# Linear attention with a gated causal unit: two tiles of 128 tokens instead of four of 64 in the raw products, and paired transposes of q in one batch

## The chip, the cores and the metric

The kernel runs on one core of a Trainium2 chip. The metric is the device time of one execution in microseconds (us); lower is better. The engines of the core are TensorE (PE; its weight loads are shown apart as PEld), VectorE (DVE), ScalarE (ACT), GpSimd (POOL) and SyncE (SP), which here only issues transfers.

## The reference

Everything is fp32. Batch 8, 8 heads, 576 tokens, head size 64, model width 512, 5 taps of a causal convolution.

```python
kv = np.einsum('bhsd,bhse->bhde', k, v)
out = np.einsum('bhsd,bhde->bhse', q, kv)
rms = np.sqrt(np.mean(out * out, axis=-1, keepdims=True) + 1e-06)
x = out / rms * g_norm                      # then heads side by side: (8, 576, 512)
for k in range(5):
    gate_pre += conv_w[k] * xp[:, k:k + S, :]   # xp: x with 4 zero tokens ahead
gate = 1.0 / (1.0 + np.exp(-gate_pre))
val = x @ w_val
return gate * val @ w_out
```

Since there is no softmax, each head needs only its 64x64 matrix kv; the "raw products" are q times that matrix, before the norm.

## The kernel before

**Order of the work.** The whole program is a list of steps written out by hand (PLAN, lines 19 to 204). Each step is a small function called with the batch and an index, such as `raw_pair 4 3`, and each engine carries out its own instructions in the order of that list. Batches overlap: while the val and out products of one batch run, the kv products and raw products of the next stand between them. An engine waits where an operand, or the PSUM bank that a step writes, isn't ready. All PSUM tiles come from eight banks that are used in turn (`ps`).

**Attention, by batch.** `kv_product` (L440) forms kv on four 64x64 quarters of TensorE; `kv_copy` brings it to SBUF (L450 for batch 0, L453 for the others). In SBUF, `kvs[b % 2]` has heads 0 to 3 on partitions 0 to 63 and heads 4 to 7 on partitions 64 to 127; the index hp (0 to 3) names such a pair of heads, and r (0 or 1) the half of the partitions. q must stand with the head dimension on the partitions: the tile qT is 128 partitions (r, d) by hp by 576 tokens. Tokens are held in an order of 18 blocks n of 32: `(n t)`.

For batches 2 to 7, `turn_q` makes qT with VectorE transposes. For batches 0 and 1, `load_q_rows` loads rows (h t) on the partitions, `turn_q_rows` (L477) turns them on TensorE for four blocks at a time (index j, 0 to 4; the last has two blocks), and `sort_q` (L484) copies the result with ScalarE from PSUM into qT, one copy for each j. In `turn_q_rows`, the matmul for block n and half r has a 128x64 weight tile (rows of q) and the 128x128 identity as moving operand, and writes to partitions r\*64 to r\*64+63: two matmuls stand side by side on the two column halves of the array.

Batch 0 multiplies by a block-diagonal kv (`raw_whole`, L512, full 128x128 weights). The other seven use `raw_product` (L501), through `raw_pair` (two chunks of 128 tokens) and `raw_tail` (the last 64 tokens). For each hp, each chunk, each 64 tokens of it (half) and each r, a 64x64 piece of qT is the weight and the 64x64 kv the moving operand. Row half r picks the PSUM bank, token half the output partitions. So four matmuls use the four quarters of the array at once.

Then `square` (L531, L535) and `sums` (L544) form the sum of squares, `powers` (L552, GpSimd) the inverse root, `normalise` the scaled x (L561 with VectorE for batch 0, L571 with ScalarE later). x is turned into xT: by TensorE (`turn_x`, L583, then `keep_x`, L590) for batches 0 and 1 and the tails, by VectorE and transfers (`turn_blocks`, `move_blocks`) for the rest.

**The gated unit.** `gate_start`, `gate_tap` (L621) and `gate_end` form the gate from xT. The product with w_val is `val_product` (L633) in batches 0 and 1, and `val_fast` (L682) after that, which saves one multiplication in eight by sums of blocks. The output product is done likewise by `fast_product` (L774) with a tail in `out_product` (L720). The weights arrive as fp64 and are narrowed to fp32 by `narrow_weight` in eight numbered parts, parts 1 to 3 on ScalarE (L368, L370, L372) and the rest on VectorE (L363, L375, L380, L385, L389), among the steps of batches 0 and 1.

**The steps around the change for batch 1** stand in this order in the list (others between them left out):

```
turn_q_rows 1 2; turn_q_rows 1 0; turn_q_rows 1 3; ... sort_q 1 0; turn_x 0 3;
turn_q_rows 1 4; sort_q 1 2; turn_q_rows 1 1; keep_x 0 3; ... sort_q 1 3; ...
turn_x 0 4; ... turn_x 0 2; ... kv_product 1 0; ... keep_x 0 2; keep_x 0 4; ...
val_product 0 1 1; ... kv_product 1 1; ... val_product 0 3 1; ...
sort_q 1 4; kv_copy 1 1; sort_q 1 1; kv_copy 1 0; ... raw_pair 1 3
```

Of the kernel before, what the change touches and what calls it, by code (L numbers as in the profile page):

```python
# [15 lines left out]
P = 128  # L16
# [191 lines left out]
def kernel(  # L208
# [11 lines left out]
    nc = tc.nc  # L220
    B, H, S, D = q.shape
    C = H * D
    HP = H // 2
    NJ = S // P
# [3 lines left out]
    TB = 32  # L228
# [4 lines left out]
    HB = P // TB  # L233
# [5 lines left out]
    TURNED_X = 2  # L239
    FAST_VAL = 2  # L240
    FAST_OUT = 0
    ROOTS = {(0, 2): H + H // 2, (0, 1): 2 * H}
    GATES = 3
    GVS = 3
# [8 lines left out]
    def ps(shape, name):  # L253
        return psum.tile(shape, FP32, tag="bank", bufs=8, name=name)

    kvs = [const.tile([P, HP, D], FP32, name=f"kv{i}") for i in range(2)]
    kv_bd = const.tile([P, HP, P], FP32, name="kvbd")
    ident = const.tile([P, P], FP32, name="ident")
# [14 lines left out]
    qs = const.tile([P, 3, NB, D], FP32, name="qs")  # L273
# [22 lines left out]
    st = {}  # L296
# [100 lines left out]
    for jt in range(NK):  # L397
        cols = slice(jt * P, (jt + 1) * P)
# [56 lines left out]
    def new_qT(b):  # L455
        if ("qT", b) not in st:
            st["qT", b] = work.tile([P, HP, S], FP32, tag="qT", name=f"qT{b}")
        return st["qT", b]
# [9 lines left out]
    def size(c):  # L468
        return P if c < NJ else T

    def turn_q_rows(b, j):

        m = min(HB, NB - j * HB)
        pq = ps([P, HB, P], f"qTps{b}_{j}")
        for n in range(m):
            for r in range(2):
                nc.tensor.matmul(  # L477
                    pq[r * D:(r + 1) * D, n, :], qs[:, r, j * HB + n, :], ident[:], start=True, stop=True)
        st["pq", b, j] = pq

    def sort_q(b, j):

        m = min(HB, NB - j * HB)
        nc.scalar.copy(  # L484
            out=new_qT(b)[:].rearrange("p h (n t) -> p n h t", t=TB)[:, j * HB:j * HB + m],
            in_=st["pq", b, j][:, 0:m].rearrange("p n (h t) -> p n h t", t=TB))

    def raw_product(b, *chunks):


        banks = [ps([P, len(chunks), C // 2 if chunks[0] < NJ else P], f"raw{b}_{chunks[0]}_{r}") for r in range(2)]
        for n, c in enumerate(chunks):
            st["raw", b, c] = [bank[:, n] for bank in banks]
        for hp in range(HP):
            for c in chunks:
                for half in range(2) if c < NJ else (hp // 2,):
                    first = c * P + (half * D if c < NJ else 0)
                    for r in range(2):
                        rows, cols = slice(r * D, (r + 1) * D), slice(half * D, (half + 1) * D)
                        to = hp if c < NJ else hp % 2  # L500
                        nc.tensor.matmul(  # L501
                            st["raw", b, c][r][cols, to * D:(to + 1) * D],
                            st["qT", b][rows, hp, first:first + D], kvs[b % 2][rows, hp, :],
                            start=True, stop=True)

    def raw_whole(b, c):

# [8 lines left out]
    def raw_pair(b, c):  # L516
        raw_product(b, c, c - 1)

    def raw_tail(b):
        raw_product(b, NJ)  # L520

    def heads(c):
        return H if c < NJ else H // 2
# [23 lines left out]
    def root_range(b, c):  # L547
        return slice(FIRST[c], FIRST[c] + ROOTS.get((b, c), heads(c)))

# [252 lines left out]
    def store(i, c, queue=nc.sync, blocks=range(HB)):  # L802
# [5 lines left out]
    steps = {f.__name__: f for f in (  # L808
        load_half, load_q, load_q_rows, stage_weight, narrow_weight, turn_cw, keep_cw, start_warm, warm_up,
        kv_product, kv_copy, turn_q, turn_q_rows, sort_q, raw_whole, raw_pair, raw_tail, square, sums, powers, normalise,  # L810
        turn_x, keep_x, turn_blocks, move_blocks, halo, gate_start, gate_tap, gate_end, val_product, keep_val, gated,
        val_sums, x_sums, val_fast, val_keep, out_product, keep_out, weight_sums, token_sums, fast_product, fast_keep,
# [36 lines left out]
```

## Time and profile before

| | us |
|---|---|
| runs shown | 304.69, 306.4, 432.16 |
| median | 306.4 |
| span of the profiled execution | 304.6 |
| TensorE time in L501 (raw products, batches 1 to 7) | 18.7 |
| TensorE time in L477 (turning q, batches 0 and 1) | 11.0 |
| ScalarE span at L484 (sorting q): 10 copies | 0.34 to 0.60 each |

A line of the profile's groups reads: source line, engine, operation, output<-inputs, for TensorE the tile of the array as rows\*columns, then the shape, the count, and after the bar the busy time in us (overlaps counted once) and the mean duration of one instruction in ns; at the end the idle time just before these instructions and what ended it. A line of the timeline reads: start in us, length in us, engine, line, operation, and how many instructions were merged into it. Matmuls are pipelined, so one instruction's duration is longer than the distance between two. The share of the core's TensorE clock that was granted is 0.993 over the span; the two lower slices lie at the start:

```profile
PEclk9979999999999999999999999999999999999999
```

### The profile page before, as it was taken

What the parts mean: (1) busy time and instruction counts of PE and PEld (TensorE: products, weight loads), DVE (VectorE), ACT (ScalarE), POOL (GpSimd) and SP (SyncE); (2) the same over time, 40 slices, a digit from 0 to 9 for tenths busy, and PEclk for the clock granted to TensorE, in tenths of its full rate; (3) what the DMA queues carried; (4) which work ended last, traced back from release to release, by engine and by line L of the source; (5) the groups of instructions that cost most, each with busy time, mean ns of one, the idle gap of its engine ahead of it and who ended that gap; (6) DMA issues with size and microseconds to landing.
All of it is one profiled execution on the core that took longest, in us unless ns stands there. A gap on an engine that the chain in (4) does not pass through costs nothing.

```text
span 304.6 us, 8977 instructions
## 1 busy us (share of the span) xinstructions
PE 294.8 (97%) x3441; PEld 232.4 (76%) x3441; DVE 269.2 (88%) x474; ACT 193.7 (64%) x596; POOL 114.9 (38%) x127
## 2 busy tenths in 40 slices
PE   7899999999999999999999999999999999999993
PEld 7788778877787785777778757787878588888582
DVE  1169999999999999999999999999999999999612
ACT  1569989999768664884586547683787354535220
POOL 3027354406568217364338352345536631000000
PEclk9979999999999999999999999999999999999999
DMA  7999998088569756988689477927411621112423
GB/s 269 343 368 343 272 302 210 4 230 269 154 147 329 231 163 167 269 220 260 173 253 294 111 175 232 326 72 214 114 48 30 169 80 34 36 42 64 103 69 103
DMA packets 32074, 55.53 MB, mean 182 GB/s; under 512 B 6166, under 2 KB 14358, under 8 KB 32032
## 3 DMA queue, kind: packets, MB, share of 16 engines
q1 hardware_dynamic: 29520, 49.76, 55.7%
q0 software_dynamic: 1632, 3.17, 4.1%
q10 hardware_dynamic: 880, 2.03, 1.8%
q8 instruction: 27, 0.44, 0.6%
q14 instruction: 15, 0.12, 0.1%
HBM read 39.21 MB, written 9.44 MB: 160 GB/s over the span
## 4 chain that ended last, share of the span: by engine, by line
PE 89%; DVE 5%; DMA 2%; issue 1%; ACT 1%; DVEq 0%; ACTq 0%; SPq 0%
PE a L774 18%; PE cb L774 14%; PE va L682 13%; PE val L633 11%; PE vc L682 6%; PE kvps L440 6%; PE raw L501 5%; PE out L720 5%; PE vb L682 4%; PE qTps L477 4%; PE raw L512 2%; PE xTps L583 2%; DMA qs<-in_q_dram 2%; DVE gate L621 2%; DVE xs L667 1%
## 5 line engine op out<-in xcount | busy, mean ns | idle before, releaser
L552 POOL TENSOR_TENSOR rt<-ss,mhalf 128x8 f32<-128x8 f32 (+3 forms) x38 | 68.9, 1822 | 101.0 <-DVE ss L544 100.8
L621 DVE SCALAR_TENSOR_TENSOR gate<-xT,cwT,gate 128x576 f32<-128x576 f32 x128 | 101.8, 809 | 1.0
L571 ACT ACTIVATE x<-raw,rt 128x64 f32<-128x64 f32 x252 | 55.8, 351 | 7.2 <-POOL rt L552 4.2
L604 POOL DMA_DIRECT2D xT<-y x48 | 26.4, 557 | 25.5 <-DVE ot L784 14.0
L633 PE MATMUL val<-xT,wval 128*128 128x288 f32 x128 | 33.0, 411 | 0.0
L774 PE MATMUL a<-wsum,sums 128*128 128x256 f32 x128 | 32.4, 382 | 0.0
L628 ACT ACTIVATE gate<-gate 128x576 f32<-128x576 f32 x32 | 22.0, 692 | 11.7 <-DVE gate L621 11.4
L633 PEld LDWEIGHTS val<-xT,wval 128*128 128x128 f32 x128 | 23.5, 190 | 6.5 <-ACT xT L590 0.4
L544 DVE TENSOR_REDUCE ss<-sq 128x8 f32<-128x520 f32 (+1 forms) x40 | 24.7, 627 | 2.9 <-ACT sq L531 2.5
L774 PEld LDWEIGHTS a<-wsum,sums 128*128 128x128 f32 x128 | 24.0, 190 | 4.1 <-issue 0.6
L535 ACT ACTIVATE sq<-raw 128x256 f32<-128x256 f32 (+1 forms) x70 | 22.4, 403 | 7.3 <-PE raw L501 7.1
L682 PE MATMUL va<-xs,vsum 128*128 128x288 f32 x96 | 26.6, 409 | 0.0
L615 ACT ACTIVATE gate<-xT,cwT 128x576 f32<-128x576 f32 x32 | 25.2, 811 | 1.5 <-DVE gv L646 1.3
L646 DVE TENSOR_TENSOR gv<-gv,gate 128x576 f32<-128x576 f32 x32 | 23.6, 750 | 0.9 <-ACT gate L628 0.8
L682 PEld LDWEIGHTS va<-xs,vsum 128*128 128x128 f32 x96 | 18.0, 190 | 5.1 <-ACT x L571 0.4
L611 POOL COPY xT<-xT 128x124 f32<-128x124 f32 x32 | 17.5, 585 | 10.5 <-ACT xT L590 10.5
L501 PEld LDWEIGHTS raw<-kv,qT 64*64 64x64 f32 x1008 | 16.4, 134 | 5.3 <-issue 3.0
L440 PEld LDWEIGHTS kvps<-v,k 64*64 64x64 f32 x1008 | 15.9, 135 | 3.7 <-issue 1.9
L501 PE MATMUL raw<-kv,qT 64*64 64x64 f32 x1008 | 18.7, 221 | 0.0
L440 PE MATMUL kvps<-v,k 64*64 64x64 f32 x1008 | 17.6, 220 | 0.0
L774 PE MATMUL cb<-wsum,sums 128*128 128x256 f32 x64 | 16.9, 386 | 0.1
L774 PE MATMUL cb<-wout,gv 128*128 128x256 f32 x64 | 16.8, 385 | 0.0
(111 smaller groups left out, 542.3 us busy)
## 6 DMA issues: line engine op xcount, KB each, us to landing
qs<-in_q_dram SPq DMA_DIRECT2D x96, 140.0 KB, 4.2
out_dram<-ot SPq DMA_DIRECT2D x140, 64.0 KB, 1.7
k<-in_k_dram SPq DMA_DIRECT2D x14, 576.0 KB, 6.3
v<-in_v_dram SPq DMA_DIRECT2D x12, 576.0 KB, 6.5
xT<-y SPq DMA_DIRECT2D x48, 64.0 KB, 2.7
xT<-y POOLq DMA_DIRECT2D x48, 64.0 KB, 3.3
y<-in_moe_w_val_dram SPq DMA_DIRECT2D x4, 512.0 KB, 11.4
w_wout<-in_moe_w_out_dram SPq DMA_DIRECT2D x4, 512.0 KB, 6.3
```

Source lines behind the costliest of these rows:

```text
L440: nc.tensor.matmul(st["kvps", b][s][r * D:(r + 1) * D, i], st["k", b, i][rows, r, cols], st["v", b, i][rows, r, cols], start=(j == 0), sto ...
L501: nc.tensor.matmul(st["raw", b, c][r][cols, to * D:(to + 1) * D], st["qT", b][rows, hp, first:first + D], kvs[b % 2][rows, hp, :], start=T ...
L544: nc.vector.reduce_sum(out=st["ss", b][:, FIRST[c]:FIRST[c] + n], in_=st["sq", b, c][:, 0:n], axis=AX.X)
L552: nc.gpsimd.tensor_tensor(out=st["rt", b][:, which], in0=st["ss", b][:, which], in1=mhalf[:, which], op=ALU.pow)
L571: nc.scalar.activation(out=x[:, to * D:(to + 1) * D], in_=raw[:, h * D:(h + 1) * D], func=AF.Copy, scale=root[:, to:to + 1])
L604: (nc.sync if i % 2 else nc.gpsimd).dma_start(out=xTs[b % 2][i * TB:(i + 1) * TB, :, first:first + P], in_=y[a * TB:(a + 1) * TB, i])
L615: nc.scalar.activation(out=gate[:], in_=xTs[b % 2][:, jt, HALO:SX], func=AF.Copy, scale=cwT[:, K - 1, jt:jt + 1])
L621: nc.vector.scalar_tensor_tensor(out=gate[:], in0=xTs[b % 2][:, jt, tap * TB:tap * TB + S], scalar=cwT[:, tap, jt:jt + 1], in1=gate[:], op ...
L633: nc.tensor.matmul(val[:], wval[:, kc, jt * P:(jt + 1) * P], xTs[b % 2][:, kc, HALO + n * SV:HALO + (n + 1) * SV], start=(kc == 0), stop=( ...
L646: nc.vector.tensor_tensor(out=both, in0=both, in1=st["gate", b, jt][:], op=ALU.mult)
L682: nc.tensor.matmul(st[bank, "val", b, mj][:], weights_[:, k], tokens()[:, k], start=(n in (0, 1, 3) and k == 0), stop=(k == NK // 2 - 1), ...
L774: nc.tensor.matmul(st[bank, i, p], tokens()[:, k], weights_[:, k], start=(n < 2 and k == 0), stop=(k == NK // 2 - 1), skip_group_check=True)
```

## The change

Two things change. The list of steps, its order and everything else stay.

In `raw_product`, a chunk of 128 tokens no longer takes two weight tiles of 64x64 for each r but one of 64x128 (64 partitions, 128 tokens). It lies on a tile of the array of half the height and the full width; two such tiles, r = 0 and r = 1, fill the array. Outputs, banks and the moving operand are the same. The tail of 64 tokens keeps its 64x64 tiles.

In `turn_q_rows` and `sort_q`, batch 1 takes another way: two neighbouring blocks n and n+1 of one r, 128 columns together, are turned by one 128x128 transpose. Its result has the even block on partitions 0 to 63 and the odd one on 64 to 127, for either r. So `sort_q` makes four copies, for each r and each parity, each from 64 partitions of PSUM to 64 partitions of qT, where it was one copy of 128 partitions.

```diff
+    PAIRED_Q = (1,)
...
-        pq = ps([P, HB, P], f"qTps{b}_{j}")
+        st["pq", b, j] = pq = ps([P, HB, P], f"qTps{b}_{j}")
+        if b in PAIRED_Q:
+            for r in range(2):
+                for n in range(0, m, 2):
+                    nc.tensor.transpose(
+                        pq[:, r * 2 + n // 2, :],
+                        qs[:, r, j * HB + n:j * HB + n + 2, :].rearrange("p n d -> p (n d)"), ident[:])
+            return
...
-        nc.scalar.copy(
-            out=new_qT(b)[:].rearrange("p h (n t) -> p n h t", t=TB)[:, j * HB:j * HB + m],
-            in_=st["pq", b, j][:, 0:m].rearrange("p n (h t) -> p n h t", t=TB))
+        qT, pq = new_qT(b)[:].rearrange("p h (n t) -> p n h t", t=TB), st["pq", b, j][:].rearrange(
+            "p n (h t) -> p n h t", t=TB)
+        if b not in PAIRED_Q:
+            nc.scalar.copy(out=qT[:, j * HB:j * HB + m], in_=pq[:, 0:m])
+            return
+        for r in range(2):
+            for e in range(2):
+                nc.scalar.copy(
+                    out=qT[r * D:(r + 1) * D, j * HB + e:j * HB + m:2],
+                    in_=pq[e * D:(e + 1) * D, r * 2:r * 2 + m // 2])
...
-                for half in range(2) if c < NJ else (hp // 2,):
-                    first = c * P + (half * D if c < NJ else 0)
-                    for r in range(2):
-                        rows, cols = slice(r * D, (r + 1) * D), slice(half * D, (half + 1) * D)
-                        to = hp if c < NJ else hp % 2
-                        nc.tensor.matmul(
-                            st["raw", b, c][r][cols, to * D:(to + 1) * D],
-                            st["qT", b][rows, hp, first:first + D], kvs[b % 2][rows, hp, :],
-                            start=True, stop=True)
+                first, to = c * P, hp if c < NJ else hp % 2
+                half = slice(0, P) if c < NJ else slice(hp // 2 * D, (hp // 2 + 1) * D)
+                for r in range(2):
+                    rows = slice(r * D, (r + 1) * D)
+                    nc.tensor.matmul(
+                        st["raw", b, c][r][half, to * D:(to + 1) * D],
+                        st["qT", b][rows, hp, first:first + size(c)], kvs[b % 2][rows, hp, :],
+                        start=True, stop=True)
```

More of the change, by code (lines that the diff above doesn't have):

```diff
@@ L478, in turn_q_rows @@
                     pq[r * D:(r + 1) * D, n, :], qs[:, r, j * HB + n, :], ident[:], start=True, stop=True)
-        st["pq", b, j] = pq
     def sort_q(b, j):
         m = min(HB, NB - j * HB)
-        nc.scalar.copy(
-            out=new_qT(b)[:].rearrange("p h (n t) -> p n h t", t=TB)[:, j * HB:j * HB + m],
-            in_=st["pq", b, j][:, 0:m].rearrange("p n (h t) -> p n h t", t=TB))
+        qT, pq = new_qT(b)[:].rearrange("p h (n t) -> p n h t", t=TB), st["pq", b, j][:].rearrange(
[8 more added lines that the diff above has]
+                    in_=pq[e * D:(e + 1) * D, r * 2:r * 2 + m // 2])
     def raw_product(b, *chunks):
```

## The prediction

> **What bounds the kernel now.** I read the page's busy time first, then its chain of waits.
>
> ```profile
> PE 294.8 (97%) x3441; PEld 232.4 (76%) x3441; DVE 269.2 (88%) x474; ACT 193.7 (64%) x596; POOL 114.9 (38%) x127
> ...
> PE 89%; DVE 5%; DMA 2%; issue 1%; ACT 1%; DVEq 0%; ACTq 0%; SPq 0%
> ```
>
> TensorE (PE) is busy for 97% of the span and is 89% of the chain. The windows view agrees: from 38 to 300 us PE is busy 260.60 of 262.00 us. So a microsecond that PE gains or loses counts fully, unless PE then waits. Both edits are PE edits: L501 (raw products) and L477 (turning q), with their copies on ScalarE (ACT) at L484.
>
> Next, the groups by line with shapes kept apart, because the change alters shapes (tile rows*columns, then operand):
>
> ```profile
> L501 PE MATMUL raw<-kv,qT 64*64 64x64 f32 x1008 | 18.7, 221 | 0.0
> L501 PEld LDWEIGHTS raw<-kv,qT 64*64 64x64 f32 x1008 | 16.4, 134 | 5.3 <-issue 3.0 <-ACT gv L642 0.8 <-DVE gv L689 0.4
> L720 PEld LDWEIGHTS out<-wout,gv 128*64 128x64 f32 x64 | 4.2, 136 | 8.0 <-issue 8.0
> L774 PEld LDWEIGHTS cb<-wout,gv 128*128 128x128 f32 x64 | 11.8, 190 | 2.1 <-ACT ot L788 0.2
> ```
>
> One fp32 matmul is two instruction pairs (load, matmul): 7 batches x 72 matmuls x 2 = 1008. A load of 64 columns takes 134 or 136 ns whether it has 64 rows or 128; one of 128 columns takes 190. The duration follows the columns, not the rows: 54 ns more for 64 more columns.
>
> How often can loads follow each other? The first loads after a change of tile shape show it, because nothing hides them. Three short stretches of the timeline (start us, us, engine, line, count):
>
> ```profile
> 89.02 0.30 PEld L774 LDWEIGHTS cb<-wout,gv 128*128 128x128 f32 x2
> 117.35 0.19 PEld L501 LDWEIGHTS raw<-kv,qT 64*64 64x64 f32 x5 [0.33 <-issue]
> 28.21 0.20 PEld L583 LDWEIGHTS xTps<-ident,x 128*128 128x128 f32 x2 [0.17 <-issue]
> ```
>
> Subtract the last load's duration from each stretch. The second 128-column load starts 0.30 - 0.19 = 0.11 us after the first. On quarters, four loads start almost together, and the fifth (the first tile's second) 0.19 - 0.13 = 0.06 us after the first. A transposing load (L583; mean 141 ns) brings 128 columns at 0.20 - 0.14 = 0.06 us.
>
> Last, how fast whole rounds run, a round being one instruction on every tile of the array (timeline of PE):
>
> ```profile
> 117.35 1.16 PE L501 MATMUL raw<-kv,qT 64*64 64x64 f32 x64
> 180.16 2.09 PE L501 MATMUL raw<-kv,qT 64*64 64x64 f32 x128
> 21.74 1.73 PE L512 MATMUL raw<-kvbd,qT 128*128 128x128 f32 x14
> ```
>
> Sixty-four more instructions, 16 rounds of four, take 2.09 - 1.16 = 0.93 us: 58 ns a round. With full-size weights and 128 moving columns (L512), (1.73 - 0.275)/13 = 112 ns each, 0.275 being one matmul's duration in that run. Streaming alone: 256 moving columns at L774 take 0.86 us for four on the chain, 216 ns each, or 0.84 ns a column, so 54 ns for 64 columns. A quarter round thus sits just above both its stream (54) and its load (55 to 60).
>
> **Raw products.** Per row pair and chunk there were 4 matmuls on 4 quarters, now 2 on 2 half-height tiles. Each instruction still streams 64 columns of kv, and two half tiles fill the array as four quarters did. So the number of rounds stays: 7 batches x 4 pairs x 4 chunks x 2 passes = 224 (896 quarter instructions divided by 4; the other 112 are the 64-token tail, which is unchanged). What changes is the load under each round: 128 columns instead of 64. It no longer fits under 54 ns of streaming, and the load sets the pace. No row shows a 64x128 load. From below a round is bounded by the stream, 54 ns; from above by two loads after each other, 2 x 107 + 5 = 219 ns. I take 112, the L512 row, where a load of the same number of columns runs at its own pace under a matmul no longer than it; the 64-row and 128-row loads of equal duration say that height doesn't help, and the quarter loads, starting together, that two tiles load side by side. Cost: 224 x (112 - 58) = +12.1 us, on PE, with no cover: PE has no waits in or right behind these stages that could absorb it.
>
> The Trainium skill has a rule for the height that no row measures directly, in "TensorE: Matmul & The Clock Gate", section "LDWEIGHTS (loading the stationary operand)": a load takes its columns divided by 1.2 GHz, and "A 32×128 weight load takes the same time as a 128×128 weight load". By it a round is 107 ns and the sum 224 x (107 - 58) = +11.0 us; it speaks against this change, and the pitches above (0.11 and 0.06 us) agree with it.
>
> **Turning q of batch 1.** Before: 36 matmuls, 72 instructions, 36 rounds of two. Rate, from the timeline of PE:
>
> ```profile
> 23.40 2.84 PE L477 MATMUL qTps<-ident,qs 128*64 128x128 f32 x48
> 26.17 0.66 PE L583 MATMUL xTps<-ident,x 128*128 128x128 f32 x4
> 26.75 1.53 PE L477 MATMUL qTps<-ident,qs 128*64 128x128 f32 x24
> 28.22 0.87 PE L583 MATMUL xTps<-ident,x 128*128 128x128 f32 x6
> ```
>
> (2.84 - 1.53)/12 = 109 ns a round, 3.9 us in all. Full transposes as in L583 need one instruction each; six take 0.87 us, (0.87 - 0.28)/5 = 0.12 us at most. The change has 18 of them: 2.0 us. It also removes three changes of tile shape around L583, about 0.15 us each (the chain gives the 24 rounds 2.77 us where 24 x 0.109 = 2.62). PE is relieved of 2.0 + 0.4 = 2.4 us.
>
> I don't expect PE to keep it. After these steps PE turns x of batch 0, which VectorE (DVE) normalises late:
>
> ```profile
> 27.45 0.42 DVE L561 TENSOR_TENSOR x<-raw,rt 128x256 f32<-128x256 f32 x1
> ...
> 29.06 1.29 DVE L561 TENSOR_TENSOR x<-raw,rt 128x512 f32<-128x512 f32 x2 [0.19 <-POOL rt L552]
> ```
>
> The x of chunk 4, the next to be turned, is ready at 27.87 (PE turned it at 28.22), and chunks 0 and 1 at 29.75 and 30.35, after roots from POOL that none of this moves; PE turned them from 30.23 on. So at 30.35 the 2.4 us have become waiting.
>
> And ACT pays. Five copies become twenty, each of half the partitions and half the elements per partition. Copies of 512 in a row take 0.49 us each (two in 1.07, one is 0.58). A copy of 256 takes 0.35 alone and one of 128 takes 0.26 (L450's 64x128 rows; 128x128 at L453 takes as much, so half the partitions save nothing). What decides is whether they overlap. On 128 partitions they do: two of 256 at L535 take 0.66, one 0.40, so 0.26 in a row. The only copies that alternate between the halves of the partitions are L450's:
>
> ```profile
> 16.56 1.09 ACT L450 COPY kvbd<-kvps 64x128 f32<-64x128 f32 x4 [1.51 <-PE kvps L440]
> ```
>
> Four in 1.09 us are 0.27 each, a whole duration: no overlap (one of them also waited for PE). With overlap the sorts cost 4 x (4 x 0.26 - 0.49) + (4 x 0.16 - 0.26) = +2.6 us, without 4 x (4 x 0.355 - 0.49) + (4 x 0.27 - 0.26) = +4.5. I take the second, as its row is the nearest in form. ACT is busy 2.87 of the 3.00 us from 30 to 33, so little of it hides. Three of these sorts stand before ACT's copies of x (L590), with one idle gap of 0.37 us:
>
> ```profile
> 26.86 0.60 ACT L590 ACTIVATE xT<-xTps 128x512 f32<-128x512 f32 x1 [0.37 <-PE xTps L583]
> 27.36 0.58 ACT L484 COPY qT<-qTps 128x512 f32<-128x512 f32 x1
> ...
> 29.97 2.04 ACT L590 ACTIVATE xT<-xTps 128x512 f32<-128x512 f32 x4
> ```
>
> 3 x 0.93 less the gap moves 29.97 to 32.4. Chunks 2 and 4, the first two of the four copies, end near 33.3, and the val product that needs them, begun at 31.16, is 2.1 us late. The exponent steps of the wval weights stand in the same queue; DVE's merge that waits for them (L375 at 30.27) slips by as much, inside PE's new delay. The last two sorts (+0.82 and +0.93) move the second kv copy, which ended at 35.46, to 39.4, and raw_pair 1 3, which PE began at 36.54 and would now reach at 38.6, waits for it until 39.4. I book +2.8 us on the path (with overlap the same steps give +1.0); bounds: -2.4 (all PE's relief kept) and +4.5 (all of ACT's extra).
>
> **Sum.** Own span 304.6 us, which is also the fastest shown run (304.69); the median is 1.8 us above. 304.6 + 12.1 + 2.8 = 319.5; I say 319, as the overlapping copies would give 317.7; that is 4.1% above the median.
>
> **Rivals.**
> - *Not slower: the half tile's load stays under the stream.* Place: L501's rounds; it decides once two 64x128 loads take under 58 ns. For: the transposing loads bring 128 columns every 60 ns, and each half tile holds only half the weights. Against: ordinary 128-column loads come every 107 ns, and a 64-row load isn't shorter than a 128-row one. Then the raw term is nil and ACT's delay remains: 304.6 + 2.8 = 307.4 us. Chance 0.09.
> - *The cost is per instruction.* If a quarter round's 58 ns were four fixed costs, half the instructions would need half; but rounds still stream 54 ns, so at most 224 x 4 = 0.9 us is won: 306.5 us with ACT's delay. Against: within a round the four start together, and two instructions on half-width tiles take 109 ns, their stream. Chance 0.02. A page names such a cost: the Trainium skill, "TensorEngine Tiling (Array Packing)", "Instruction Overhead", about 60 cycles for each matmul however small. By it four take 100 ns at the 2.4 GHz that the skill's TensorE page gives, and the measured 58 disagrees.
> - *Worse: loads lose their cover or queue for each other.* Load and stream in turn: 107 + 54 = 161 ns, +23 us, 330 us; one load after the other: 219 ns, +36 us, 343 us. Against: in all three shapes in the rows load and stream overlap. Chance 0.05.
>
> **How the numbers follow.** The forecast has 0.84. Its range: 304.6 + 12.1 - 2.4 = 314 up to 306.4 + 12.1 + 4.5 = 323, the upper end from the median run. It leaves out 0.16 in the rivals, and little more, so I keep it. Faster by over 2% (6 us; about what a measurement of this kernel can tell from no change) needs the relief kept and loads hidden, even then 302: 0.01. Within 2%, the two rivals: 0.11. Slower: 0.88.
>
> **What would show it.** L501 should have 560 instructions, 448 of them 64*128 with loads near 190 ns and rounds of two near 112 ns; a stage of 64 instructions that took 1.16 us becomes one of 32 near 2.0 us. L477 keeps batch 0's 72, and 18 transposes appear; ACT has 20 copies of batch 1, near 0.355 us apart (0.26 if they overlap), and PE waits before the val product and raw_pair 1 3. I am wrong if 64*128 loads come every 60 ns, or if PE is early at raw_pair 1 3.

## The result, and the profile after

The changed kernel takes 317.38 us (median of 4 runs, 316.67 to 318.26), the kernel before 305.54: the ratio is 1.0393 [1.0358, 1.0429], slower. Of the four runs of the kernel before (304.67, 304.69, 306.4 and 432.16 us), the last, a slow one, is left out of the ratio; without it their median is 304.69, and the change costs 12.7 us. The profiled execution has a span of 315.3 us and took 317.07.

The page after, busy time and chain of waits:

```profile
PE 301.8 (96%) x2939; PEld 241.0 (76%) x2939; DVE 270.8 (86%) x474; ACT 197.4 (63%) x611; POOL 114.8 (36%) x127
...
PE 81%; DMA 7%; ACT 7%; SPq 1%; issue 1%; DVE 0%; ACTq 0%; DVEq 0%
```

TensorE (PE) runs 502 instruction pairs fewer and is busy 7 us longer. ScalarE (ACT) is now 7% of the chain instead of 1%; the transfers (DMA) are 7% instead of 2%, for loads of q and v. The groups by line, shapes kept apart (raw products are now at L514, turning by transposes at L479, the sort at L498):

```profile
L514 PE MATMUL raw<-kv,qT 64*128 64x64 f32 x448 | 27.4, 274 | 0.4 <-ACT kv L454 0.4
L514 PEld LDWEIGHTS raw<-kv,qT 64*128 64x128 f32 x448 | 25.9, 188 | 4.4 <-issue 2.0 <-ACT kv L454 1.2 <-ACT x L584 0.4
L479 PE MATMUL qTps<-ident,qs 128*128 128x128 f32 x18 | 3.0, 323 | 1.4 <-ACT qT L498 1.4
L498 ACT COPY qT<-qTps 64x256 f32<-64x256 f32 x16 | 5.8, 365 | 0.2
```

A load of the new shape takes 188 ns, as long as the 128x128 loads of before (190): half the rows save nothing. The rate of rounds is in PE's timeline (start, length, engine, line, count):

```profile
122.83 2.00 PE L514 MATMUL raw<-kv,qT 64*128 64x64 f32 x32
...
188.35 3.79 PE L514 MATMUL raw<-kv,qT 64*128 64x64 f32 x64
```

Thirty-two more instructions, 16 rounds of two, take 3.79 - 2.00 = 1.79 us: 112 ns a round, where the quarters had 58. How often a load can start is seen at the head of such a stage, in PEld's timeline up to the third load:

```profile
122.83 0.29 PEld L514 LDWEIGHTS raw<-kv,qT 64*128 64x128 f32 x3 [0.33 <-issue]
```

The first two, one on each tile, start together, and the third, the first tile's second, 0.29 - 0.19 = 0.10 us after them (108 ns in the trace). So the two tiles load side by side, and each takes nearly a whole round for its 128 columns. Now the turning of batch 1, PE and then ACT:

```profile
20.65 1.47 PE L479 MATMUL qTps<-ident,qs 128*128 128x128 f32 x12
22.57 0.63 PE L596 MATMUL xTps<-ident,x 128*128 128x128 f32 x4 [0.45 <-ACT sq L544]
...
24.59 1.52 PE L479 MATMUL qTps<-ident,qs 128*128 128x128 f32 x6 [1.38 <-ACT qT L498]
26.11 1.54 PE L596 MATMUL xTps<-ident,x 128*128 128x128 f32 x6
...
31.27 2.21 PE L646 MATMUL val<-xT,wval 128*128 128x288 f32 x8 [0.86 <-ACT xT L603]
...
37.26 2.41 PE L514 MATMUL raw<-kv,qT 64*128 64x64 f32 x48 [0.43 <-ACT kv L454]
```

```profile
23.04 3.02 ACT L498 COPY qT<-qTps 64x256 f32<-64x256 f32 x8
...
26.58 1.49 ACT L498 COPY qT<-qTps 64x256 f32<-64x256 f32 x4
...
30.35 1.85 ACT L603 ACTIVATE xT<-xTps 128x512 f32<-128x512 f32 x4
...
36.94 0.27 ACT L454 COPY kv<-kvps 128x128 f32<-128x128 f32 x1
```

PE turns q faster and then waits three times for ACT: at 24.59 for a PSUM bank that the sort copies must free, at 31.27 for xT, at 37.26 for the kv copy. (The wait at 22.57 is put down to ACT too, but VectorE (DVE) wrote the x that PE turns there until 22.43.) From 21.48 to 37.22 us the chain of waits runs through ACT alone. Eight copies take 3.02 us; less the last one's 0.37 that is (3.02 - 0.37)/7 = 0.38 us from start to start, so they don't overlap.

Where the time went is read from the start of the same PE step in both timelines. The kernel before has, beside the turning of q that the prediction shows:

```profile
31.16 2.11 PE L633 MATMUL val<-xT,wval 128*128 128x288 f32 x8
...
36.54 1.44 PE L501 MATMUL raw<-kv,qT 64*64 64x64 f32 x80
```

| step | before | after | later by |
|---|---|---|---|
| first turning of batch 1 | 23.40 | 20.65 | -2.7 |
| first val product of batch 0 | 31.16 | 31.27 | +0.1 |
| raw_pair 1 3 | 36.54 | 37.26 | +0.7 |
| end of the span | 304.6 | 315.3 | +10.7 |

So the stretch from the turning to raw_pair 1 3 took 16.61 us instead of 13.14: +3.5. From there on each of the 14 raw_pair steps adds 0.84 us, 11.8 together. Some 1.8 us are given back in pieces of 0.05 to 0.3 us, in small waits of the kernel before (at 63.8, 143 and 157 us, for instance). The head of before's profile happened to be late, part of it because the clock was halved from 17.3 to 20.8 us (the 7 in before's clock line, its only lower slice). The sum: 304.6 - 2.7 + 3.5 + 11.8 - 1.8 = 315.4, against a span of 315.3.

### The profile page after: what moved, and what is told of

Same layout as the page of the kernel before. It is cut to its first block, busy times and chain, and to the rows that moved or that the text cites. A ratio compares the mean times of both kernels' runs of the same rounds, so it can differ in the third digit from the quotient of the medians.

```text
span 315.3 us, 7982 instructions
## 1 busy us (share of the span) xinstructions
PE 301.8 (96%) x2939; PEld 241.0 (76%) x2939; DVE 270.8 (86%) x474; ACT 197.4 (63%) x611; POOL 114.8 (36%) x127
## 4 chain that ended last, share of the span: by engine, by line
PE 81%; DMA 7%; ACT 7%; SPq 1%; issue 1%; DVE 0%; ACTq 0%; DVEq 0%
PE a L787 18%; PE cb L787 13%; PE va L695 13%; PE val L646 9%; PE raw L514 9%; PE vc L695 6%; PE kvps L441 5%; PE out L733 5%; DMA qs<-in_q_dram 4%; PE vb L695 4%; DMA v<-in_v_dram 3%; ACT qT L498 2%; PE xTps L596 1%; ACT wexp_wval L369 1%; ACT xT L603 1%
## 5 line engine op out<-in xcount | busy, mean ns | idle before, releaser
L514 PEld LDWEIGHTS raw<-kv,qT 64*128 64x128 f32 (+1 forms) x560 | 28.3, 177 | 5.8 <-issue 3.4
L514 PE MATMUL raw<-kv,qT 64*128 64x64 f32 (+1 forms) x560 | 30.6, 265 | 0.4 <-ACT kv L454 0.4
L624 POOL COPY xT<-xT 128x124 f32<-128x124 f32 x32 | 17.3, 581 | 13.6 <-ACT xT L603 13.6
L787 PE MATMUL a<-wsum,gv 128*128 128x256 f32 x64 | 16.7, 384 | 0.0
L797 DVE TENSOR_TENSOR ot<-cb,ot 128x512 f32<-128x512 f32 x16 | 10.9, 682 | 6.8 <-DMA out_dram<-ot 4.1
```

What stands on the lines that cost most here:

```text
L514: nc.tensor.matmul(st["raw", b, c][r][half, to * D:(to + 1) * D], st["qT", b][rows, hp, first:first + size(c)], kvs[b % 2][rows, hp, :], s ...
L787: nc.tensor.matmul(st[bank, i, p], tokens()[:, k], weights_[:, k], start=(n < 2 and k == 0), stop=(k == NK // 2 - 1), skip_group_check=True)
```

## The experiments

Theory: the round is paced by its 128-column load, and ACT's separate copies set the turning section. Rivals: the stream or a fixed cost sets the round; the turning costs by its relief or by something else.

**raw_only: the half-height products alone.**

```diff
-    PAIRED_Q = (1,)
+    PAIRED_Q = ()
```

> The raw products on half-height tiles alone; q of batch 1 is turned and sorted as before. Theory (a 128-column load sets the round at 112 ns instead of 58): 448 instructions on 64*128 with loads near 190 ns, a stage of 32 of them near 2.0 us instead of 1.16 us for 64, +10 to +12 us over before (about 315 to 317 us). Rival (most of the loss comes from the turning and sorting of q): less than +5 us, under 311 us.

Measured: 315.9 us against 305.06, ratio 1.0376 [1.0313, 1.0439], +10.8 us, as expected. The raw products are the main cost. Behind the head, PE's timeline also has one long stall that no engine explains (in brackets: the wait ahead and its releaser; "issue" is none):

```profile
109.75 0.42 PE L514 MATMUL raw<-kv,qT 64*64 64x64 f32 x7
111.57 0.45 PE L514 MATMUL raw<-kv,qT 64*64 64x64 f32 x9 [1.40 <-issue]
```

**wide_moving: the changed kernel with 128 columns streamed instead of 64** (for hp 0 to 2; the surplus half is overwritten).

```diff
+                    w = 2 if c < NJ and hp < HP - 1 else 1
...
-                        st["raw", b, c][r][half, to * D:(to + 1) * D],
-                        st["qT", b][rows, hp, first:first + size(c)], kvs[b % 2][rows, hp, :],
+                        st["raw", b, c][r][half, to * D:(to + w) * D],
+                        st["qT", b][rows, hp, first:first + size(c)],
+                        kvs[b % 2][rows, hp:hp + w, :].rearrange("p h e -> p (h e)"),
```

> As the changed kernel, but for row pairs 0 to 2 each raw matmul of a full chunk streams 128 columns of kv instead of 64 (this pair's and the next one's; the next pair's own matmul then overwrites the surplus), so 168 of 224 rounds stream twice as much under the same load. Theory (the load paces the round): streaming 107 ns still fits under it, rounds stay near 112 ns, the time equals the changed kernel's 317 us within 1 us. Rival (streaming, or writing columns into two banks, paces a round on half-height tiles): 168 x 54 ns = +9 us, 326 us.

Measured: 318.26 us, ratio 1.0428 [1.0391, 1.0464]. The stage of 64 instructions, 48 of them with twice the columns, is unchanged to the last digit:

```profile
92.34 3.79 PE L515 MATMUL raw<-kv,qT 64*128 64x128 f32 x64
```

Twice the streaming is free, so the stream doesn't set the round; the load does. The profiled execution is 1.5 us longer than the changed kernel's, and all of that lies ahead of the raw products: raw_pair 1 3 starts at 38.78 instead of 37.26, and from there to the end both take 278.0 us (316.8 - 38.78 and 315.3 - 37.26).

**sort_parts: when do ACT's copies overlap?** The kernel before, with batch 1's five full copies cut up in three ways.

```diff
+        parts = {
+            (1, 0): ((low, 0), (low, 2), (up, 0), (up, 2)),
+            (1, 2): ((low, 0), (up, 0), (low, 2), (up, 2)),
+            (1, 1): ((whole, 0), (whole, 2))}.get((b, j))
...
+        for (p0, p1), n in parts:
+            nc.scalar.copy(out=qT[p0:p1, j * HB + n:j * HB + n + 2], in_=pq[p0:p1, n:n + 2])
```

> The kernel before, with three of batch 1's five sorting copies cut into parts of two blocks: j=0 in the order lower half, lower, upper, upper of the partitions; j=2 lower, upper, lower, upper; j=1 on all 128 partitions, two copies. Theory (copies overlap unless the range of partitions changes): starts 0.26 us apart within a range and on 128 partitions, 0.36 us where the range changes. Rival 1 (copies of 64 partitions never overlap): 0.36 us throughout j=0 and j=2. Rival 2 (they overlap as any others and the sorts of the changed kernel were slow for another reason, the crossing of halves or the strided output): 0.26 us throughout.

Measured, from start to start in the trace: low after low 256 ns, up after up 272, whole after whole 264; but low to up 379, up to low 392, and alternating 378, 378 and 377. In ACT's timeline, cut after the second and after the third copy of the first way:

```profile
23.95 0.62 ACT L496 COPY qT<-qTps 64x256 f32<-64x256 f32 x2
...
23.95 1.00 ACT L496 COPY qT<-qTps 64x256 f32<-64x256 f32 x3
```

The second copy adds 0.26 us to the first's 0.36, the third, which changes to the other partitions, 0.38. Copies overlap by about 0.11 us unless the range of partitions changes; both rivals fall. In these parts input and output change range together. In the changed kernel each copy reads other partitions than the one before, and every second one still writes to the same: starts are 365 to 393 ns apart all the same, so a change of the input alone is enough. Whether a change of the output alone is, no run shows. The whole kernel took 306.07 us in its one run.

**turn_only: the transposes and their sorting copies alone**, with the raw products of before.

```diff
-                half = slice(0, P) if c < NJ else slice(hp // 2 * D, (hp // 2 + 1) * D)
...
+                for half in range(2) if c < NJ else (hp // 2,):
+                    first = c * P + (half * D if c < NJ else 0)
```

> The paired transposes and the four sorting copies of batch 1 alone; raw products on quarters as before. Theory (20 copies that follow each other 0.37 us apart hold up ScalarE, and PE's relief turns into waiting): raw_pair 1 3 starts 3 us or more after the place where it stood before, counted from the first turning of batch 1; the total is +1.5 to +3.5 us over before, since later waits give some back. Rival (PE keeps its relief of 2.4 us): 0 to -2.4 us.

Measured: 313.95 us, ratio 1.0306 [1.0257, 1.0355]: +8.9 us, a miss. With raw_only's 10.8 the parts add to 19.7, where both together cost 11.8 (12.7 against 304.69). The stretch to raw_pair 1 3 grew by 4.1 us, near the theory; the rest of the excess in the trace is stalls without a releaser, the longest inside raw products that the edit doesn't touch:

```profile
38.81 1.38 PE L515 MATMUL raw<-kv,qT 64*64 64x64 f32 x75
42.11 0.38 PE L515 MATMUL raw<-kv,qT 64*64 64x64 f32 x5 [1.91 <-issue]
...
113.26 0.28 PE L441 MATMUL kvps<-v,k 64*64 64x64 f32 x3 [0.98 <-issue]
```

Such a stage had run through in 1.44 us. The transfers give a hint: queue q8, of kind "instruction", moves 16 KB at a time, once per 256 records of PE (27 times for about 7,000). Counted from 0 over PE's records in the trace (loads, matmuls and semaphore events), PE resumes at record 1216 and at record 3264; both are 192 + 256 k. raw_only's stall ends at 3008, again 192 + 256 k. New theory: PE waits for its own next block of instructions; which work is hit depends on its number alone. Rival: the new copies or transfers disturb these stages.

**side_1: the relief without the many copies.** The kernel before, with q of batch 1 loaded so that one 128x128 transpose serves both r; ACT keeps its five copies.

```diff
+        return qs[:, 0:2].rearrange("p r n d -> p (r n d)").rearrange("p (n r d) -> p n r d", r=2, d=D)
...
+                nc.tensor.transpose(pq[:, n, :], side_by_side()[:, j * HB + n].rearrange("p r d -> p (r d)"), ident[:])
```

> The kernel before, with the rows of q of batch 1 loaded so that both halves r of a block lie side by side (in pieces of 256 bytes); one 128x128 transpose then turns both at once into the old layout, so five sorting copies stay as they were. PE is relieved of 2.4 us, ScalarE pays nothing. Theory (PE's relief turns into waiting for VectorE's x of batch 0, so it was never worth anything): 305 us, within 1 us of before. Rival (only ScalarE's copies ate the relief): -2 to -2.4 us, 303 us. If the short pieces load late, slower than before by what the first turn of batch 1 waits.

Measured: 310.33 us against 304.7, ratio 1.0208 [1.0157, 1.026]; a miss. Stalls again:

```profile
31.42 0.68 PE L450 MATMUL kvps<-gv 64*64 64x64 f32 x28
33.90 0.92 PE L450 MATMUL kvps<-gv 64*64 64x64 f32 x44 [1.80 <-issue]
...
39.98 0.34 PE L514 MATMUL raw<-kv,qT 64*64 64x64 f32 x5 [1.72 <-issue]
```

They end at records 960 and 1216; a third, at 3264, is of 1.3 us.

**turn_pad and turn_shift: only the numbers moved.** turn_pad is turn_only with 27 small matmuls far ahead of it, in the step of the convolution weights; turn_shift is turn_only with a longer warm-up (`start_warm` 44 instead of 36).

```diff
+        for _ in range(27):
+            nc.tensor.matmul(cwps[0:TB, :], ident[:, 0:TB], ident[:, 0:NK * K + 1], start=True, stop=True)
```

> turn_only with 27 small matmuls (54 instruction pairs, overwritten by the transpose that follows them) put into an idle stretch of PE before L415, so that from there on PE's instructions have the same numbers as in the kernel before. Theory (part of turn_only's loss is PE waiting for its own instructions in the dense 64x64 stages, where a block of them happens to end): no stalls of 1 to 2 us without a releaser inside the raw and kv stages; the time falls from 314 to about 309 or 310 us, which is the waits of the sorts alone. Rival (those stalls are waits for data or for a bank, or chance): unchanged, 313 to 315 us.

> turn_only with 8 more warm-up matmuls (16 instruction pairs) at the start. Theory (a stall stands where a block of PE's instructions ends): the stall that turn_only showed with 5 matmuls left of the raw tail of batch 1 stands about 16 matmuls earlier, with about 21 left, in the end of the raw pair 1 3 or the start of the tail. Rival (it is a wait of the raw tail for something): with 5 left again, or none.

Measured: turn_pad 309.21 us, ratio 1.0159 [1.0123, 1.0194]; with 108 instructions more it is 4.5 us above the kernel before, where turn_only was 8.9 above. turn_shift 308.59 in its one run. In turn_shift the stall did not move 16 matmuls earlier, as the theory had it; it was gone, for a reason that the last section gives. raw_pair 1 3 of turn_pad runs through, after a wait that has its cause:

```profile
38.41 1.44 PE L517 MATMUL raw<-kv,qT 64*64 64x64 f32 x80 [0.41 <-ACT kv L456]
```

The transposes and copies are the same as in turn_only, so the rival falls. Turning alone costs about 4 to 4.5 us without the stalls.

**side_pad: side_1 with the same 27 matmuls.**

> side_1 with the same 27 small matmuls as in turn_pad, so that PE's later instructions have their old numbers. side_1 took 310.3 us and its profile has three stalls of 1.5 to 2.0 us without a releaser in kv and raw stages, two of them at the places where turn_only had them. Theory (both kernels lack the same 108 instructions of PE, and the ends of its blocks fall there): the stalls are gone, 305 us, no difference from before beyond 1 us either way, since PE's relief turns into waiting for VectorE. Rival (the short pieces of the load or the transposes themselves cost the 5 us): 309 to 311 us.

Measured: 304.76 us against 304.25, ratio 1.0016 [0.9993, 1.0039]. With the stalls gone, PE's relief is worth nothing: it has become waits. PE's timeline, and the one long wait with a releaser that side_1 has at the same step (waits: us in total, times, longest):

```profile
22.94 0.63 PE L598 MATMUL xTps<-ident,x 128*128 128x128 f32 x4 [0.45 <-ACT sq L546]
24.04 1.14 PE L489 MATMUL qTps<-ident,qs 128*128 128x128 f32 x6 [0.47 <-ACT qT L499]
26.18 0.85 PE L598 MATMUL xTps<-ident,x 128*128 128x128 f32 x6 [0.99 <-ACT wexp_wval L378]
```

```profile
PE xTps L596 <- DVE x L574: 0.8, 1, 0.8
```

The longest wait, at 26.18, is for the x that VectorE (DVE) writes until 26.03 us. The profile names an ACT instruction that ends 0.04 us later and writes exponents of the weights, which PE doesn't read here; in side_1 it names DVE. The wait at 22.94 is of the same kind (x until 22.79); the one at 24.04 is for a sort copy of ACT.

**before_shift: the kernel before, with 37 small matmuls** in that place, which gives its later steps the numbers modulo 256 that they have in turn_only.

> The kernel before with 37 small matmuls (148 instructions) in the idle stretch before L414, so that PE's later instructions stand, modulo 256, as in turn_only and side_1; nothing else differs. Theory (blocks of 256 PE instructions): stalls of 1 to 2 us with 5 matmuls left of the raw tail of batch 1 and in the kv products of batch 4, 308 to 310 us. Rival (the stalls belong to what turn_only and side_1 do with q): 305 us, plus at most the 1 us by which the small matmuls could overrun the idle stretch.

Measured: 315.01 us, ratio 1.0353 [1.0311, 1.0395]: +10.8 us from 148 instructions in the head. The direction is as expected, the size beyond it. PE's timeline:

```profile
15.70 0.51 PE L442 MATMUL kvps<-v,k 64*64 64x64 f32 x19
19.00 0.39 PE L442 MATMUL kvps<-v,k 64*64 64x64 f32 x11 [2.78 <-issue]
...
39.27 1.38 PE L503 MATMUL raw<-kv,qT 64*64 64x64 f32 x76
42.45 0.33 PE L503 MATMUL raw<-kv,qT 64*64 64x64 f32 x4 [1.80 <-issue]
...
116.17 0.28 PE L442 MATMUL kvps<-v,k 64*64 64x64 f32 x3 [1.85 <-issue]
```

The stalls end at records 704, 1472 and 3520, all 192 + 256 k, and sum to 6.4 us. The second hits raw_pair 1 3 almost where turn_only has it, in a kernel without any of the change. The span grew from 304.6 to 313.2 us; beside the stalls, 1.7 us of that is a halved clock that follows the second one (last section).

None of these versions is faster than the kernel before.

## Why the prediction came out right, and where it didn't

- **The raw round: right.** 112 ns as taken from the L512 row; loads 188 ns (190), a stage of 32 in 2.00 us (2.0). The term was 12.1 us; the steps sum to 11.8. The measured round refutes the first rival (under 58 ns) and the third (161 or 219 ns); that twice the streaming is free speaks against load and stream in turn as well. The second falls too: half the instructions, nearly twice the time. The rule for loads that it weighed (the Trainium skill, "TensorE: Matmul & The Clock Gate", section "LDWEIGHTS (loading the stationary operand)") gives 107 ns whatever the height; the trace agrees on the height, and 112 is 5 ns above it.
- **"No cover": wrong by about 1.8 us.** The prediction saw no waits in or right behind the stages. There were small ones further on, in before's own steps, and they took up that much.
- **PE's relief is worth nothing: right**, and side_pad shows it by itself. The longest of its waits is the one that the prediction named, for the x of batch 0 that VectorE (DVE) writes; another is for ACT. In the changed kernel itself ACT's copies are later than that x, and they set the section.
- **ACT's copies: right in kind, small in size.** No overlap, 0.38 us apart for the 0.355 booked. From the start of the turning, the first val product is 2.9 us later (2.1 booked) and raw_pair 1 3 is 3.5 us later (2.8 booked). Not foreseen was the wait of 1.38 us at the second turning, for a bank that the sort copies free; the longer distance between copies adds to it.
- **The base: wrong, and hidden by luck.** The prediction took the profiled span, 304.6, for the fastest shown run. In every run here the device time is 1.8 us above the span (317.07 and 315.3; 312.0 and 310.2), so the profiled execution is the one of 306.4, and its head was late. On its own base the sum would have been 306.4 + 14.9 = 321.3. That base was too high by about as much, since the kernel before had medians of 304.25 to 305.06 in the later comparisons.
- **Two terms were missing**: where the blocks of instructions end, and the halved clock. In the changed kernel the first happens to cost next to nothing: behind the head its profile lists no wait of PE's matmuls without a releaser. The second is hidden in the turning section. That is luck: turn_only shows how the same forecast would have failed for one part of the change, +8.9 us where +2.8 was booked.

The parts can be told apart by the time from raw_pair 1 3 to the end of the span: 268.1 us in the kernel before, 278.0 in the changed kernel and in wide_moving, 279.7 in raw_only, which has a stall of 1.4 us there. The raw products cost about 10 us net in all three, the stall aside. Open: neither raw_only nor the changed kernel was run with other numbers, so what those would cost there is not shown.

## What to carry to other kernels

Before a tile of half the height is chosen to save instructions, compare the load of its columns with the stream under it: four 64-column loads side by side kept up with 64 moving columns (58 ns), two 128-column loads did not (112 ns). When one copy becomes several, keep those that read and write the same partitions together, and count what the copying engine does next. Before a difference of 1 to 4% is put down to an edit, shift the instruction numbers by a few dozen small instructions elsewhere and measure again, or see in the trace whether an instruction transfer landed shortly before PE resumed.

## What the hardware showed that was not expected

**Blocks of 256 instructions.** In these kernels, every stall of PE of about 1 us or more without a releaser in the body of a kernel ended at a record 192 + 256 k (seven different places in turn_only, side_1, before_shift and raw_only), and 148 instructions in the head of an unchanged kernel cost 10.8 us. While the first two stalls of before_shift last, the 16 DMA engines are fully busy; around the third they are not (windows: stretch, its length, busy time of PE, PEld, DVE, ACT and POOL with counts, granted clock, DMA share, GB/s):

```profile
15.90:19.20 3.30, 0.52 (x30) 0.38 (x23) 2.53 (x6) 0.00 (x0) 0.00 (x0) 1.00 1.03 389
39.00:43.00 4.00, 2.20 (x83) 1.73 (x82) 3.96 (x8) 3.68 (x9) 0.00 (x0) 1.00 1.02 306
113.00:117.00 4.00, 2.15 (x111) 1.92 (x103) 4.00 (x8) 2.24 (x11) 0.00 (x0) 1.00 0.42 118
```

Shown is that the place follows the number and that padding brings or removes the loss. That PE waits there for its own instructions is inferred from the order of events: counted from the start, each 16 KB transfer of q8 belongs to one end of a block. In the eleven traces PE passes none of the 276 such ends less than 1.2 us after its transfer has landed, and the nine stalls end 1.2 to 1.6 us after it (40.66 and 42.11 us in turn_only). This also tells why most ends cost nothing: their transfer had landed earlier. In turn_shift it landed at 37.38 us, and PE came to that end at 39.09, late enough not to wait. No run changed the transfers themselves. The Trainium skill, "Runtime: NRT & Kernel Launch", section "Instruction fetch mechanics", tells of blocks of 16 KiB with 256 instructions, and calls the cost of crossing one "mostly hidden"; the trace agrees on the block, and here the cost was not hidden.

**The clock can halve after a half-idle stretch.** The granted clock falls to 0.50 for 3.41 us, or twice that, by the trace's clock records. The windows of the changed kernel, the stretch ahead and the halved one:

```profile
21.40:24.80 3.40, 1.57 (x12) 1.12 (x11) 3.32 (x7) 3.34 (x9) 3.40 (x3) 0.98 1.06 400
24.80:28.00 3.20, 3.19 (x14) 2.33 (x13) 2.87 (x6) 3.11 (x9) 2.01 (x1) 0.50 1.08 384
```

PE had been busy 1.57 of 3.40 us. The six transposes of x that then ran at half clock took 1.54 us instead of 0.87. It cost nothing in the end: turn_shift, with no such stretch, needs the same 16.61 us from the turning to raw_pair 1 3 (21.60 to 38.21), because ACT sets that time. Where it lasted twice as long, in turn_only and wide_moving, that section took 17.23 us. In before_shift, where the stall left PE idle, it costs:

```profile
40.40:43.80 3.40, 1.60 (x24) 1.18 (x16) 3.37 (x7) 3.12 (x8) 0.00 (x0) 0.98 1.01 339
43.90:47.10 3.20, 3.20 (x8) 2.34 (x7) 3.09 (x6) 1.06 (x3) 3.17 (x2) 0.50 1.06 278
```

All of that stretch is work of PE, and the next step starts 1.7 us later. The kernel's own waits don't always trigger it: turn_shift was busy 1.50 of the 3.40 us from 23.5 us on and kept its clock. The Trainium skill, "TensorE: Matmul & The Clock Gate", section "Part 1: The HAM clock gate", gives a free-running window of 3,413 ns, which agrees with the length of these stretches and would explain why the same idle time is met in one run and not in another. The traces agree: within each, all changes of the clock lie whole multiples of 3.413 us apart. Marked off in such steps, PE's idle time in the changed kernel falls into one step (busy 1.59 of 3.42 us from 21.23), in turn_shift into two (2.50 of 3.41 from 21.21, 1.84 from 24.62). Where the limit lies isn't shown: of the steps with PE busy 44 to 55%, some are followed by a halved one and some are not.

**ACT's copies.** Two copies of 256 elements per partition with the same range of partitions start 256 to 272 ns apart in sort_parts, two of different ranges 377 to 392 ns.
